# Hashed attention with a mixture of adapters: sign rows read over 16 partitions, loads behind them, and a new order for the first pair

## The chip, the cores and the metric

The kernel runs on one core of one Trainium2 chip. The metric is the device time of one execution in microseconds (us). A profile of one execution gives the span from its first to its last instruction, which is a little shorter: 193.1 us in an execution of 195.3 us.

## The reference, cut to what matters

Attention over 4 batches x 8 heads with 768 positions of 64 dimensions. Queries and keys are hashed to six bits each, and a query sees only keys with the same six bits. The output of all heads, 3072 rows of 512, then goes through a top-2 mixture of eight rank-16 adapters.

```python
q_bits = (np.einsum('bhsd,dk->bhsk', q, proj) > 0)        # proj: 64 x 6
k_bits = (np.einsum('bhsd,dk->bhsk', k, proj) > 0)
mask   = q_bucket[:, :, :, None] == k_bucket[:, :, None, :]
scores = np.where(mask, scale * q @ k.T, -1e9)
attn   = softmax(scores)                                  # sum + 1e-09
out    = attn @ v
# ... then, on x = out as 3072 x 512:
logits = x @ w_gate                                       # 8 experts, the best 2 are taken
delta  = sum over the 2 of  w * ((x @ A[e]) @ B[e])
return x + delta
```

## The kernel before: the parts that the change touches

The heads are taken in 16 pairs. For a pair, `aug` holds queries and keys, transposed, in rows 0 to 63, and six rows of signs (+ or - times a scale) and one constant row in rows 64 to 70. One matmul over 71 rows then gives the score plus a large negative number wherever a bit differs, so the mask costs nothing more, and the exponential turns those to zero. `aug[:, t, h, i, :]` is row block t (6 of them), head h, and i = 0 for queries, 1 for keys.

A pair is nine steps `s`. Each step makes 1024 columns of scores, an exponential on ScalarE, and carries other work along: that of the pair before (values, normalisation, adapters) and of the next two pairs (loads, casts, transposes, hashes, signs).

```python
def score(self, p, s, ...):
    ps = self.ps_s.tile([P, 1024], F32, tag="s", ...)
    # 2 or 3 matmuls of 256 or 512 columns:
    nc.tensor.matmul(out=ps[:, o:o + w], lhsT=aug[0:71, kt, h, 1, :], rhs=aug[0:71, ..., h, 0, :], ...)
    nc.scalar.activation(out=self.P_[p][:, s * 1024:end], in_=ps, func=ACT.Exp, ...)
```

The signs of a later pair take a way through memory. `turn32` transposes 32 x 32 blocks on VectorE, `hash` multiplies by the projection on TensorE, `sign` makes the signs on VectorE and writes them to a scratch tensor in device memory, and `signs` reads them back into rows 64 to 70 of `aug`:

```python
def sign(self, p, r0=0, r1=128):
    # ... signs into s2, [128, T, 32] bf16
    if p not in self.dr:
        self.dr[p] = self.scr.tile([T, P, 32], BF16, tag="dr", name=f"dr{p}")
    nc.sync.dma_start(out=self.dr[p].rearrange("t p c -> p t c")[r0:r1], in_=s2[r0:r1])

def signs(self, p, js=None):
    aug = self.aug[p % 3]
    if js is None:
        nc.sync.dma_start(out=aug[64:71].rearrange("b t h i c -> b (t h i) c"),
                          in_=self.dr[p].rearrange("t (j b i) c -> b (t j) (i c)", j=4, b=8)[0:7])
        return
    # ... else one of four quarters at a time
```

Queries and keys come by `loadqk` (384 KB each), are cast to bf16 by GpSimd (`natcast`), and transposed by a DMA (`xbar`) into all 128 rows of the head-0 half of `aug`, of which rows 64 to 127 are head 1. `shift`, on VectorE, moves these to rows 0 to 63 of the head-1 half, and only after it may the sign rows be written.

```python
def slot(self, p, s):
    n1, n2 = p + 1, p + 2
    self.score(p, s)
    if p == 0: self.first(s)
    self.pvs(p - 1, s + 9); self.pvs(p, s)
    if p > 0:
        if s in (0, 1): self.hash(n1, s)
        if s == 2: self.sign(n1)
        if s == 3:
            self.norm(p - 1, 1); self.to_bf(p - 1); self.shift(n1)
        if s == 4: self.signs(n1)
        if s == 6: self.turn(p - 1)
        if s == 2: self.loadv(n1)
    if s in (5, 6):
        self.natcast(n2, s - 5); self.xbar(n2, s - 5)
    if s == 7:
        self.loadqk(p + 3, 0); self.loadqk(p + 3, 1)
    # ... turn32 of n2 at 5 and 6, vcast of n1 at 7, norm(p, 0) at 8, the adapters
    if s == 3 and p >= 8 and p % 4 < 3:
        self.store(p // 4 - 2, p % 4)                     # 512 KB of output
```

All these DMAs are issued by SyncE, in the order in which they stand here, and SyncE waits in that order too.

Pair 0 has no pair before it, so `start` and `first` make its transposes and hashes on TensorE directly from the loads; `cast` fills rows 0 to 63 and `sign_here` the sign rows, on VectorE, one instruction for every half `e` of the row blocks. Here j = 0, 1 are queries and keys of head 0 and j = 2, 3 those of head 1.

```python
def first(self, s):
    v = self.hb if s else None
    if s == 0:
        v = self.hb = [self.ps_v.tile([self.P, 512], F32, tag="v", ...) for e in range(2)]
        self.cast(0, 2, "act"); self.hash_here(2, v)
        self.turn32(1, 0, 0); self.turn32(1, 1, 0)
    if s == 1:
        self.cast(1, 2, "act"); self.hash_here(3, v)
        self.sign_here(2, 0, v[0]); self.sign_here(2, 1, v[1])
    if s == 2:
        for f in range(2): self.hash(1, f, (0, 1))
        self.sign(1, 0, 64); self.loadv(1)
        self.sign_here(3, 0, v[0], 0, 1); self.sign_here(3, 1, v[1], 0, 1)
    if s == 3:
        self.turn32(1, 0, 1); self.turn32(1, 1, 1); self.shift(1)
        self.signs(1, (0, 1))
        self.sign_here(3, 0, v[0], 1, 3); self.sign_here(3, 1, v[1], 1, 3)
    if s == 4:
        for f in range(2): self.hash(1, f, (2, 3))
        self.sign(1, 64, 128)
    if s == 6: self.signs(1, (2, 3))
```

Of the kernel before, what the change touches and what calls it, by code (L numbers as in the profile page):

```python
# [12 lines left out]
F32 = mybir.dt.float32  # L13
# [6 lines left out]
class Emitter:  # L20


    def __init__(self, ctx, tc, q, k, v, proj, w_gate, A, Bm, out):
# [27 lines left out]
        self.sgp = pool("sgp", 2)  # L51
        self.scr = ctx.enter_context(tc.tile_pool(name="scr", bufs=2, space=bass.MemoryType.DRAM))
        self.pp = pool("pp", 2)
# [11 lines left out]
        self.nat, self.vn, self.P_, self.pv = {}, {}, {}, {}  # L65
        self.tr, self.hs, self.R, self.nb, self.dr = {}, {}, {}, {}, {}
        self.x, self.xb, self.xT, self.lz = {}, {}, {}, {}
# [3 lines left out]
    def consts(self):  # L71
        nc, P, T, D, S = self.nc, self.P, self.T, self.D, self.S
        sg = self.singles
        self.wz = sg.tile([P, 512], BF16, name="wz")
        nc.vector.memset(self.wz, 0.0)
        self.dume = sg.tile([P, 1], F32, name="dume")
        nc.scalar.activation(out=self.dume, in_=self.wz[:, 0:1], func=ACT.Exp)
        self.ident = sg.tile([P, P], F32, name="ident")
        make_identity(nc, self.ident)
        self.proj3 = sg.tile([P, 32], F32, name="proj3")  # L80
        nc.vector.memset(self.proj3, 0.0)
        self.aug = [sg.tile([P, T, 2, 2, P], BF16, name=f"aug{i}") for i in range(3)]
        self.vb = [sg.tile([P, 2, T + 1, D + 1], BF16, name=f"vb{i}") for i in range(3)]
        for j in range(4):
            nc.vector.memset(self.aug[0][64:96, :, j // 2, j % 2, :], 1.0 if j % 2 == 0 else -1.5)
        self.eps = sg.tile([P, P], BF16, name="eps")
        nc.gpsimd.memset(self.eps, 2.0 ** -56)
        self.ident_bf = sg.tile([P, P], BF16, name="ident_bf")
        nc.gpsimd.tensor_copy(out=self.ident_bf, in_=self.ident)
        self.wa = sg.tile([P, self.nD, self.LZ], BF16, name="wa")  # L90
        self.Bcat = sg.tile([self.ER, self.Dm], BF16, name="Bcat")

# [94 lines left out]
    def sign(self, p, r0=0, r1=128):  # L187
# [7 lines left out]
        nc.vector.tensor_scalar(out=s2[r0:r1], in0=sg, scalar1=self.ssc[r0:r1], scalar2=None, op0=ALU.mult)  # L195
        if p not in self.dr:
            self.dr[p] = self.scr.tile([T, P, 32], BF16, tag="dr", name=f"dr{p}")
        nc.sync.dma_start(out=self.dr[p].rearrange("t p c -> p t c")[r0:r1], in_=s2[r0:r1])

    def signs(self, p, js=None):  # L200
# [4 lines left out]
        if js is None:  # L205
            nc.sync.dma_start(out=aug[64:71].rearrange("b t h i c -> b (t h i) c"),
                              in_=self.dr[p].rearrange("t (j b i) c -> b (t j) (i c)", j=4, b=8)[0:7])
            return
        src = self.dr[p].rearrange("t (j b i) c -> b j t (i c)", j=4, b=8)[0:7]
        for j in js:  # L210
            nc.sync.dma_start(out=aug[64:71, :, j // 2, j % 2, :], in_=src[:, j])

# [57 lines left out]
    def sign_here(self, j, e, tile, u0=0, u1=3):  # L270
        r = 64 + 32 * (j % 2)
        self.nc.vector.tensor_scalar(out=self.augv(slice(64, 70), j, e)[:, u0:u1],
                                     in0=tile[r:r + 6, 0:384].rearrange("p (u c) -> p u c", u=3)[:, u0:u1],
                                     scalar1=0.0, scalar2=0.5, op0=ALU.is_gt, op1=ALU.subtract)

# [257 lines left out]
    def start(self):  # L533
# [7 lines left out]
        self.loadqk(0, 0, 1, nc_s)  # L541
        self.loadqk(0, 1, 1, nc_a)
        self.loadqk(1, 0)
        self.loadqk(1, 1)
# [8 lines left out]
        h = [self.ps_s.tile([self.P, 2, 512], F32, tag="s", name=f"h{j}") for j in range(2)]  # L553
        h = [(t[:, 0], t[:, 1]) for t in h]
        for j in (0, 1):
            for u in range(3):
                self.T1(j, u, j == 1)
        warm(1)
        self.tcopy(0)
        self.tcopy(1, "act")  # L560
        self.hash_here(0, h[0])
        self.hash_here(1, h[1])
        self.cast(0, 0)
        self.cast(1, 0, "act")
        self.cast(0, 1, "act")
        self.cast(1, 1, "act")
        self.sign_here(0, 0, h[0][0])
        self.sign_here(0, 1, h[0][1])
        self.sign_here(1, 0, h[1][0], 0, 1)
        self.sign_here(1, 1, h[1][1], 0, 1)  # L570
        for j in (2, 3):
# [12 lines left out]
        self.vcast(0)  # L584
        self.sign_here(1, 0, h[1][0], 1, 3)
        self.sign_here(1, 1, h[1][1], 1, 3)

    def first(self, s):
        v = self.hb if s else None
        if s == 0:  # L590
            v = self.hb = [self.ps_v.tile([self.P, 512], F32, tag="v", name=f"hb{e}") for e in range(2)]
            self.cast(0, 2, "act")
            self.hash_here(2, v)
            self.turn32(1, 0, 0)
            self.turn32(1, 1, 0)
        if s == 1:
            self.cast(1, 2, "act")
            self.hash_here(3, v)
            self.sign_here(2, 0, v[0])
            self.sign_here(2, 1, v[1])  # L600
        if s == 2:
            for f in range(2):
                self.hash(1, f, (0, 1))
            self.sign(1, 0, 64)
            self.loadv(1)
            self.sign_here(3, 0, v[0], 0, 1)
            self.sign_here(3, 1, v[1], 0, 1)
        if s == 3:
            self.turn32(1, 0, 1)
            self.turn32(1, 1, 1)  # L610
            self.shift(1)
            self.signs(1, (0, 1))
            self.sign_here(3, 0, v[0], 1, 3)
            self.sign_here(3, 1, v[1], 1, 3)
        if s == 4:
            for f in range(2):
                self.hash(1, f, (2, 3))
            self.sign(1, 64, 128)
        if s == 6:
            self.signs(1, (2, 3))  # L620

    def pvs(self, p, s):
# [5 lines left out]
        if p == 0:  # L628
            own = {6: [(A, -1), (A, 0), (A, 1)], 7: [(A, 2), (A, 3)], 8: [(A, 4), (A, 5)],
                   9: [(B, -1), (B, 0), (B, 1)], 10: [(B, 2), (B, 3)], 11: [(B, 4), (B, 5)]}  # L630
        for (d, h), k in own.get(s, ()):
# [5 lines left out]
    def slot(self, p, s):  # L637
# [6 lines left out]
        if p > 0:  # L644
            if s in (0, 1):
                self.hash(n1, s)
            if s == 2:
                self.sign(n1)
            if s == 3:
                self.norm(p - 1, 1)  # L650
                self.to_bf(p - 1)
                self.shift(n1)
            if s == 4:
                self.signs(n1)
            if s == 6:
                self.turn(p - 1)
            if s == 2:
                self.loadv(n1)
        if s in (5, 6):
            self.natcast(n2, s - 5)  # L660
            self.xbar(n2, s - 5)
        if s == 7:
            self.loadqk(p + 3, 0)
            self.loadqk(p + 3, 1)
        t = 4 if n2 == self.N - 1 else 5
# [4 lines left out]
        if n2 == self.N - 1:  # L670
# [4 lines left out]
            if s == 8:  # L675
                self.sign(n2)
                self.vcast(n2)
        if (p, s) == (1, 0):
            self.norm(0, 0)
        if s == 8 and p > 0:  # L680
            self.norm(p, 0)
        if p > 0:
            self.moe(p, s)
        if s == 3 and p >= 8 and p % 4 < 3:
            self.store(p // 4 - 2, p % 4)

# [26 lines left out]
    def late(self, g):  # L713
# [11 lines left out]
        if g == 2:  # L725
            self.shift(q)
            self.signs(q)
            self.store(b - 2, 2)
        if g == 3:
# [140 lines left out]
```

## Time and profile before

| | before |
|---|---|
| device time, median of three (lowest, highest) | 196.92 us (193.67, 197.64) |
| span of the profiled execution | 193.1 us |
| ScalarE busy | 149.2 us, 77% |
| TensorE busy (PE) | 169.9 us, 88% |
| VectorE busy | 119.3 us, 62% |
| GpSimd busy | 100.3 us, 52% |
| DMA queue of SyncE, share of 16 engines | 69.3% |
| mean granted TensorE clock | 0.885 |

PE is matmuls, PEld the weight loads that overlap them, DVE is VectorE, ACT ScalarE, POOL GpSimd, SP SyncE. A "q" after the name stands for the engine's sequencer, which waits and issues DMAs. In a group of instructions, "out<-in" names the tiles written and read; after the bar come busy time, mean nanoseconds of one, then the idle time of the engine just before these instructions and what ended most of it. A matmul at a lower granted clock counts as busy for longer, so a busy PE is not a PE at its peak. The span falls into a start up to the first exponential at 8.77 us, fourteen pairs of nine steps, 18 steps for the last two pairs together (from 160.7 us), and a tail after the last exponential of them (from 179.3 us).

### The profile page before, as it was taken

To read this page: it belongs to the slowest core of one execution; us is meant where nothing else is said; L and a number is where in the kernel's file an instruction comes from. 1 tells how busy PE (TensorE), PEld (TensorE's weight loads), DVE (VectorE), ACT (ScalarE), POOL (GpSimd) and SP (SyncE) were. 2 spreads that over 40 slices of the span, in tenths; PEclk is the share of its full clock that TensorE was granted. 3 is DMA by queue.
4 is the path that set the end of the run, shared out by engine and by line. 5 is a ranking of instruction groups with operands and counts; after the bars stand their busy time and mean duration, and the time that the engine had idled before them with its cause. 6 is when DMAs were issued, how large, how long until landed. Compare 5 with 4: busy or idle time off the path is not lost.

```text
span 193.1 us, 5252 instructions
## 1 busy us (share of the span) xinstructions
PE 169.9 (88%) x2116; PEld 110.9 (57%) x2116; DVE 119.3 (62%) x331; ACT 149.2 (77%) x170; POOL 100.3 (52%) x148
## 2 busy tenths in 40 slices
PE   7989989897999999899959999699978999989750
PEld 3425665665466758475735767367552677879410
DVE  7879564645144767687934487476880728586750
ACT  3797897989567999898955799658993489988540
POOL 3798276959374465556551906446171475111190
PEclk9999999999657999999995899958995589999955
DMA  5864588999979687876994998947597591415025
GB/s 156 289 208 99 128 248 222 154 210 142 198 153 119 208 124 240 102 243 107 283 219 132 240 194 202 253 102 100 164 225 218 111 250 26 160 70 219 2 109 221
DMA packets 58542, 33.06 MB, mean 171 GB/s; under 512 B 44310, under 2 KB 56726, under 8 KB 58518
## 3 DMA queue, kind: packets, MB, share of 16 engines
q1 hardware_dynamic: 53254, 31.80, 69.3%
q0 software_dynamic: 4832, 0.27, 4.6%
q10 hardware_dynamic: 432, 0.66, 0.9%
q8 instruction: 16, 0.26, 0.6%
q14 instruction: 8, 0.07, 0.1%
HBM read 20.06 MB, written 7.03 MB: 140 GB/s over the span
## 4 chain that ended last, share of the span: by engine, by line
PE 65%; DMA 17%; ACT 8%; DVE 4%; issue 2%; POOL 1%; POOLq 1%; SPq 0%; DVEq 0%; ACTq 0%
PE s L299 31%; DMA aug<-dr 14%; PE pv L330 13%; PE hs L183 8%; ACT P L306 6%; DMA dr<-s 3%; PE lz L433 3%; PE dl L502 3%; PE pv L318 2%; PE warm L551 2%; PE xtp L369 1%; PE pv_u L387 1%; ACT acc L512 1%; ACT aug L258 1%; PE hb L266 1%
## 5 line engine op out<-in xcount | busy, mean ns | idle before, releaser
L306 ACT ACTIVATE P<-s 128x1024 bf16<-128x1024 f32 x144 | 139.8, 1027 | 29.7 <-PE s L299 28.6
L299 PE MATMUL s<-aug 71*128 71x256 bf16 (+1 forms) x408 | 95.4, 342 | 12.2 <-DMA aug<-dr 10.0
L330 PEld LDWEIGHTS <-P 128*128 128x128 bf16 x1008 | 49.9, 103 | 16.7 <-issue 4.8
L299 PEld LDWEIGHTS <-aug 71*128 71x128 bf16 x408 | 34.8, 102 | 35.6 <-issue 14.3
L330 PE MATMUL pv<-vb,P 128*128 128x65 bf16 x1008 | 52.8, 201 | 0.0
L359 POOL CAST xb<-x 128x768 bf16<-128x768 f32 x14 | 16.5, 1177 | 56.6 <-DVE x L350 53.8
L173 DVE STREAM_TRANSPOSE R<-nat 128x768 f32<-128x768 f32 (+1 forms) x32 | 29.1, 918 | 1.3 <-DMA nat<-in_q_dram 0.9
L219 POOL CAST nb<-nat 128x768 bf16<-128x768 f32 x30 | 24.4, 836 | 1.5 <-DMA nat<-in_k_dram 0.9
L192 DVE TENSOR_SCALAR hs<-hs 128x192 f32<-128x192 f32 (+1 forms) x16 | 5.8, 362 | 24.6 <-PE hs L183 24.5
L183 PE MATMUL hs<-R,hst 128*32 128x192 f32 x240 | 18.6, 366 | 0.3 <-DVE R L173 0.3
L515 DVE SCALAR_TENSOR_TENSOR acc<-dl,rt,x 128x512 f32<-128x512 f32 x20 | 14.6, 739 | 5.0 <-PE dl L502 4.9
L159 POOL CAST vb<-vn 128x768 bf16<-128x768 f32 x16 | 13.3, 830 | 6.7 <-DMA vn<-in_v_dram 6.3
L350 DVE TENSOR_TENSOR x<-pv,ri 128x384 f32<-128x384 f32 x28 | 15.6, 558 | 1.0
L370 DVE COPY xT<-xtp 128x768 bf16<-128x768 bf16 x14 | 7.8, 556 | 13.3 <-PE xtp L369 13.0
L161 POOL TENSOR_TENSOR vs<-vn 128x384 f32<-128x384 f32 x16 | 15.9, 993 | 0.0
L502 PE MATMUL dl<-Bcat,zT 128*128 128x512 bf16 x24 | 10.1, 437 | 2.2 <-ACT zT L493 0.8
L433 PE MATMUL lz<-wa,xT 128*128 128x136 bf16 x96 | 10.7, 242 | 0.7 <-ACT xT L422 0.5
L183 PEld LDWEIGHTS hs<-R,hst 128*32 128x32 f32 x240 | 5.5, 112 | 8.7 <-issue 6.6
L318 PE MATMUL pv<-vb,eps 128*128 128x390 bf16 x28 | 10.1, 361 | 0.0
L233 DVE COPY aug<-aug 64x1536 bf16<-64x1536 bf16 x15 | 8.9, 595 | 0.5
L409 POOL CAST xb<-x 128x256 bf16<-128x256 f32 x5 | 2.0, 400 | 12.3 <-DVE x L406 12.3
L164 POOL TENSOR_TENSOR vb<-vs,vs 128x128 bf16<-128x128 f32 x16 | 7.3, 457 | 1.3
(70 smaller groups left out, 141.1 us busy)
## 6 DMA issues: line engine op xcount, KB each, us to landing
vn<-in_v_dram SPq DMA_DIRECT2D x16, 384.0 KB
nat<-in_q_dram SPq DMA_DIRECT2D x15, 384.0 KB
nat<-in_k_dram SPq DMA_DIRECT2D x15, 384.0 KB
out_dram<-acc SPq DMA_DIRECT2D x10, 512.0 KB
out_dram<-acc SPq DMA_DIRECT2D x3, 256.0 KB
dr<-s SPq DMA_DIRECT2D x14, 48.0 KB
aug<-dr SPq DMA_DIRECT2D x14, 42.0 KB
aug<-nb SPq DMA_TRANSPOSE x30
```

Of the source, the lines that this page charges most:

```text
L161: nc.gpsimd.tensor_add(out=s3, in0=vn[:, :, 0:3, :], in1=vn[:, :, 3:6, :])
L173: self.nc.vector.transpose(out=self.R[p][:, i, hs, :], in_=self.nat[p][:, i, hs, :])
L183: nc.tensor.matmul(out=self.hs[p][32 * j:32 * j + 32, 0:6], lhsT=self.hst[:, hf].rearrange("p b i -> p (b i)"), rhs=rhs, start=(hf == 0), ...
L219: self.nc.gpsimd.tensor_copy(out=self.nb[p][:, i].rearrange("p t h d -> p h t d"), in_=self.nat[p][:, i].rearrange("p h (t d) -> p h t d", ...
L299: nc.tensor.matmul(out=ps[:, o:o + w], lhsT=aug[0:71, kt, h, 1, :], rhs=rhs, start=True, stop=True)
L306: nc.scalar.activation(out=self.P_[p][:, s * 1024:end], in_=ps, func=ACT.Exp, scale=128.0 if p == 0 else 0.125)
L330: self.nc.tensor.matmul(out=pv[:, i, :], lhsT=self.P_[p][:, o:o + P], rhs=vb[:, h, kt, :], start=False, stop=(kt == T - 1), skip_group_che ...
L350: nc.vector.tensor_tensor(out=self.x[b][:, :, c:c + D], in0=pv[:, :, 0:D], in1=ri.unsqueeze(2).to_broadcast([P, T, D]), op=ALU.mult)
L359: self.nc.gpsimd.tensor_copy(out=xb, in_=self.x[b][:, :, hp * P:(hp + 1) * P])
L433: nc.tensor.matmul(out=self.lz[b, I][:, I.index(i), :], lhsT=self.xT[b][:, t, i, :], rhs=self.wa[:, t, :], start=(t == 0 and i == I[0]), s ...
L502: self.nc.tensor.matmul(out=ps, lhsT=self.zT[b, i][0], rhs=self.Bcat, start=True, stop=True)
L515: nc.vector.scalar_tensor_tensor(out=acc, in0=dl, scalar=rt, in1=x, op0=ALU.mult, op1=ALU.add)
```

## The change

It has two sides. For the pairs from 1 on, the read of the sign rows takes 16 partitions of `aug` (64 to 79) instead of 7, from a scratch tensor that has one more row so that the last partitions have something to read; rows 71 to 79 are not used by any matmul. The order on SyncE's queue changes with it: the loads of q and k for three pairs ahead come right behind the sign read and ahead of the two transposes, and the store of output moves from between sign write and sign read to the end of the pair before. The shift stands ahead of the normalisation. This is to keep other transfers out of the way of the sign read, which the next pair's first score needs.

For pair 0, the two hash products of head 1 are made one after the other, into different rows of the same two tiles, and all of head 1's signs are made ahead of pair 1's; the signs of head 0 become one instruction for both halves; a cast goes from ScalarE to VectorE. Pair 1's second head is hashed and read later, and the value matmuls of pairs 0 and 1 move by about a step. One warm-up matmul is left out.

```diff
-        self.scr = ctx.enter_context(tc.tile_pool(name="scr", bufs=2, space=bass.MemoryType.DRAM))
+        self.scr = ctx.enter_context(tc.tile_pool(name="scr", bufs=1, space=bass.MemoryType.DRAM))
+        self.drs = [self.scr.tile([T + 1, P, 32], BF16, name=f"dr{i}") for i in range(2)]
 ...
-        nc.sync.dma_start(out=self.dr[p].rearrange("t p c -> p t c")[r0:r1], in_=s2[r0:r1])
+        nc.sync.dma_start(out=self.drs[p % 2][0:T].rearrange("t p c -> p t c")[r0:r1], in_=s2[r0:r1])
+
+    def drsrc(self, p):
+        a = self.drs[p % 2][0:1].rearrange("o p c -> o (p c)")
+        return bass.AP(a.tensor, a.offset, [[128, 16], [1024, 4 * self.T], [1, 128]])
 ...
-            nc.sync.dma_start(out=aug[64:71].rearrange("b t h i c -> b (t h i) c"),
-                              in_=self.dr[p].rearrange("t (j b i) c -> b (t j) (i c)", j=4, b=8)[0:7])
+            nc.sync.dma_start(out=aug[64:80].rearrange("b t h i c -> b (t h i) c"), in_=self.drsrc(p))
 ...  (the quarters of pair 1: 16 partitions for queries, 7 for keys)
 ...  (start)
-        warm(1)
-        self.sign_here(0, 0, h[0][0])
-        self.sign_here(0, 1, h[0][1])
-        self.sign_here(1, 0, h[1][0], 0, 1)
-        self.sign_here(1, 1, h[1][1], 0, 1)
+        self.sign_here(0, None, h[0])
+        self.sign_here(1, None, h[1], 0, 1)
 ...  (first)
         if s == 0:
-            self.cast(0, 2, "act")
-            self.hash_here(2, v)
         if s == 1:
+            self.hash_here(2, v)
+            self.hash_here(3, v)
             self.cast(1, 2, "act")
-            self.hash_here(3, v)
+            self.cast(0, 2)
             self.sign_here(2, 0, v[0])
             self.sign_here(2, 1, v[1])
+            self.sign_here(3, 0, v[0], 0, 1)
+            self.sign_here(3, 1, v[1], 0, 1)
         if s == 2:
             for f in range(2):
                 self.hash(1, f, (0, 1))
+            self.sign_here(3, 0, v[0], 1, 3)
+            self.sign_here(3, 1, v[1], 1, 3)
             self.sign(1, 0, 64)
 ...
-            self.signs(1, (0, 1))
+            self.signs(1, (1, 0))
+            self.loadqk(3, 0)
-        if s == 4:
+        if s == 6:
             for f in range(2):
                 self.hash(1, f, (2, 3))
             self.sign(1, 64, 128)
-        if s == 6:
-            self.signs(1, (2, 3))
+            self.loadqk(3, 1)
+        if s == 8:
+            self.signs(1, (3, 2))
 ...  (pvs: the value matmuls of pair 0 start at step 7 instead of 6 and end at 12, those of pair 1 follow)
 ...  (slot)
             if s == 2:
                 self.sign(n1)
+                self.loadv(n1)
             if s == 3:
+                self.shift(n1)
+            if s == (3, 4)[p == 1]:
                 self.norm(p - 1, 1)
                 self.to_bf(p - 1)
-                self.shift(n1)
 ...
         if s in (5, 6):
+            if s == 5 and p > 0:
+                self.loadqk(p + 3, 0)
+                self.loadqk(p + 3, 1)
             self.natcast(n2, s - 5)
             self.xbar(n2, s - 5)
-        if s == 7:
-            self.loadqk(p + 3, 0)
-            self.loadqk(p + 3, 1)
 ...
-        if s == 3 and p >= 8 and p % 4 < 3:
-            self.store(p // 4 - 2, p % 4)
+        if s == 8 and n1 >= 8 and n1 % 4 < 3:
+            self.store(n1 // 4 - 2, n1 % 4)
 ...  (late: one store taken out, since slot does it)
```

## The prediction

> **What bounds the kernel now.** I read the page first: slices, then groups. In the slices the row PEclk shows the TensorE clock that was granted; in the groups two lines matter, the exponentials on ScalarE (L306) and the score matmuls (L299).
>
> ```profile
> PEclk9999999999657999999995899958995589999955
> L306 ACT ACTIVATE P<-s 128x1024 bf16<-128x1024 f32 x144 | 139.8, 1027 | 29.7 <-PE s L299 28.6
> L299 PE MATMUL s<-aug 71*128 71x256 bf16 (+1 forms) x408 | 95.4, 342 | 12.2 <-DMA aug<-dr 10.0
> ```
>
> The reader is to see three things. The 144 exponentials are 139.8 us of a 193.1 us span, so ScalarE is the engine that could fill the span. It stood idle 28.6 us because scores were late. The scores were late for 10.0 us because the sign rows of `aug` had not been read back (`aug<-dr`). And the clock falls to a half or so in four stretches in the middle.
>
> The third view is the timeline of ScalarE, which gives the start of each pair's first exponential, and from it the windows of one pair each (start:end, length, then busy time of PE, PEld, DVE, ACT and POOL, then granted clock, DMA share, GB/s). Pairs 5 to 9:
>
> ```profile
> 62.30:71.35 9.05, 9.02 (x140) 6.12 (x132) 5.82 (x21) 8.87 (x12) 5.46 (x7) 1.00 0.81 172
> 71.35:80.64 9.29, 8.55 (x131) 6.13 (x127) 7.33 (x29) 8.72 (x11) 5.44 (x7) 1.00 0.85 183
> 80.64:89.70 9.06, 8.88 (x129) 5.85 (x126) 7.59 (x15) 8.64 (x9) 4.74 (x6) 1.00 0.72 169
> 89.70:100.67 10.97, 8.82 (x128) 5.73 (x124) 7.36 (x14) 8.66 (x10) 6.14 (x9) 1.00 1.03 221
> 100.67:112.85 12.18, 12.15 (x141) 7.66 (x140) 5.83 (x20) 8.93 (x11) 5.45 (x7) 0.72 0.86 176
> ```
>
> A pair in which nothing goes wrong takes 9.05 to 9.29 us, with ScalarE busy 8.6 to 8.9 of it. Pair 8 has the same work on every engine and takes 10.97. Pair 9 takes 12.18 with PE busy all through at clock 0.72: there TensorE is the bound, because it is slow. So the end is set by ScalarE where all goes well, by a sign read at the head of a pair, or by a slow TensorE after it. The fourth view, the chain of waits around the end of pair 8, and the fifth, SyncE's queue in it, show which:
>
> ```profile
> 94.23 0.45 PE s L299 x3
> 94.93 4.99 DMA aug<-dr
> 99.97 0.61 PE s L299 x3
> ```
>
> ```profile
> 92.44 0.37 SPq L198 DMA_DIRECT2D dr<-s  x1
> 92.84 0.55 SPq L151 DMA_DIRECT2D vn<-in_v_dram  x1
> 93.44 0.47 SPq L531 DMA_DIRECT2D out_dram<-acc  x1
> 94.93 0.29 SPq L206 DMA_DIRECT2D aug<-dr  x1
> 95.32 2.79 SPq L225 DMA_TRANSPOSE aug<-nb  x2
> 98.17 1.13 SPq L143 DMA_DIRECT2D nat<-in_q_dram  x1
> 99.34 0.46 SPq L143 DMA_DIRECT2D nat<-in_k_dram  x1
> ```
>
> The sign read is issued at 94.93, behind a 384 KB load of V and a 512 KB store, with two DMA transposes 0.4 us behind it, and the next pair's scores start at 99.97. In pair 1 (26.91) and pair 2 (36.13) the same read, without a store, took 2.41 and 2.39 us in the chain; in pair 7 3.31; in the three pairs with a store ahead and the wait visible 4.99, 5.09 and 5.46.
>
> **What the Trainium skill says.** "TensorE: Matmul & The Clock Gate", section "HAM oscillation — how this bites in real kernels": a TensorE gap longer than about 3.4 us brings the clock back to half. The trace fits: the chain's waits of 4.99 us (94.93), 5.09 us (117.68), 5.46 us (140.20) and the 3.16 + 3.57 us of write and read at 41.74 to 48.54 are each followed by a window of clock 0.61 to 0.72, and those of 2.4 and 3.3 us are not. (TensorE still has some work in these gaps, so the fit is in which gaps, not in a bare length.) "DMA: Bandwidth & Descriptors", section "Why a DMA increments its semaphore by 16 and not by 1": a queue spreads a transfer over the largest number of engines up to 16 that divides the slowest dimension, so 7 partitions use 7 engines and 16 use 16. The trace does not name engines, so no view here shows it. Same page, section "Queues, rings and completion order": an engine takes descriptors in order, and the completion mark lands only after that engine's earlier writes. So what stands ahead of the sign read in the queue, and on the same engines, delays it; 2.4 us against 5 us with a store ahead agrees.
>
> **The change, part by part.** (a) *Order on SyncE.* Per pair the queue was sign write, V load, (store), sign read, transpose, transpose, q load, k load. It becomes sign write, V load, sign read, q load, k load, transpose, transpose, (store). No work is added but bytes: the read grows from 42.0 KB to 16 x 24 x 256 B = 98 KB, the same 24 pieces per partition. I work out a pair from its first score at 0. The sign write is issued at about +3.3 (32.53 - 29.36 = 3.2 in pair 2, 92.44 - 89.05 = 3.4 in pair 8) and its read follows 1.5 to 3.6 us later, when the write has landed (66.67 - 64.56 = 2.1; 36.13 - 32.53 = 3.6). So the read is issued at +5.4 to +6.9 and, at 2.4 us, ready at +7.8 to +9.3. A pair is 9.15 us long. So with nothing heavy ahead and no transposes close behind, the read is just in time nearly always. (b) *Stores* go out at the end of the pair before, some 2 us ahead of the next sign write; 512 KB at the 400 GB/s that the DMA view shows around 96 us is 1.3 us of transfer, mostly over by then.
>
> The gain: pairs 2 to 13 take, from the ScalarE timeline, 160.7 - 30.07 = 130.6 us. At (9.21 + 9.05 + 9.29 + 9.06) / 4 = 9.15 us they would take 109.8. So 20.8 us at most: the waits at the heads of pairs, and the slow clock that follows four of them (49.30 to 62.30 took 13.00 us, 100.67 to 112.85 took 12.18, 123.52 to 135.75 took 12.23, 146.84 to 160.70 took 13.86).
>
> (c) *Pair 0.* Its nine exponentials take 8.77 to 19.85 = 11.08 us. Two lines, of ScalarE and of VectorE:
>
> ```profile
> 16.10 4.71 ACT L306 ACTIVATE P<-s 128x1024 bf16<-128x1024 f32 x5 [1.15 <-PE s L299]
> 15.83 0.77 DVE L272 TENSOR_SCALAR aug<-hb 6x256 bf16<-6x256 f32 x2
> ```
>
> ScalarE waited 1.15 us for scores that waited for the last signs of head 1, queued on VectorE behind pair 1's signs, transposes and shift. These signs now come first, both hash products one after the other, and one of two casts (0.52 us each on ScalarE) goes to VectorE. That is 1.15 + 0.52 = 1.7 us less on ScalarE; the two merged sign instructions for head 0 save VectorE perhaps 0.3 us more. In return pair 1's second-half signs are hashed at step 6 instead of 4 and read at step 8 instead of 6; they are used in the middle of pair 1. I count 1.2 us gained. (d) *Pair 1* took 10.22 us, of which 0.98 was the wait in front of pair 2: 0.8 us gained.
>
> The most that can be had is thus 20.8 + 1.2 + 0.8 = 22.8 us. I take off 0.3 us in each of the twelve pairs (3.6 us) for reads that come at +9.3 rather than +7.8, and 3 us for one slow-clock stretch that stays (a stretch like pair 9 costs 12.18 - 9.15 = 3.0). That leaves 16.2 us. The last two pairs (18.6 us for 18 exponentials) and the tail (13.80 us after 179.3) are as before. 196.92 - 16.2 = 180.7; I say 180.
>
> **The rivals.** *A late transpose takes the place of the late sign read.* The transposes now stand behind 768 KB of loads. If the loads are issued at +6 and take 3.7 us, the transposes land at about +12, that is +3 in the next pair, and the shift that needs them stood at +4 (33.38 - 29.36). VectorE's order has the shift ahead of the normalisation now, so a late shift also delays the bf16 copy, the next cast on GpSimd and so the next transpose: a loop from pair to pair. For it: the DMA view shows about 1.4 us near 99 in which next to nothing is moved, with transposes in flight. Against it: VectorE has 1.5 to 4 us idle in each pair and no idle time before the shift is listed now. It would make some 0.5 to 1 us a pair, time 186 to 190. *The read is no faster, only wider.* More than twice the bytes, on all engines instead of few, waits for the slowest of them. Then the non-store pairs stay as they are and only the three stores gain, with the clock stretches behind them: about (10.97 - 9.15) + (10.67 - 9.15) + (11.09 - 9.15) = 5.3 us plus 3 x 3 us, time 183. *The clock falls anyway.* If TensorE's slow stretches come from something else than these waits, 20.8 shrinks by the excess of pairs 4, 9, 11 and 13, 3.9 + 3.0 + 3.1 + 4.7 = 14.7, and only some 6 us are won, time 191.
>
> **Range and chances.** All clean gives 196.92 - 22.8 = 174; the worst rival that I believe 191. I put the 80% range at 172 to 190. The executions before lie between 193.67 and 197.64, so even the third rival would be near 3% faster. Faster by over 2%: 0.88; within 2%: 0.08; slower: 0.04, for a loop of late transposes worse than I see.
>
> **What would show it right or wrong.** Right: PE's wait for `aug<-dr` falls from 10.0 to under 3 us; the windows of pairs 2 to 13 come near 9.15 us each; the granted clock stays at 1.00 between 20 us and the last pairs; ScalarE's wait on scores falls from 28.6 to about 12 us; the 1.15 us in pair 0 is gone. Wrong: new idle time on VectorE ahead of the shift ended by `aug<-nb`, a read that still takes 4 to 5 us in the chain, or half-clock stretches that no wait precedes.

## The result and the profile after

| | before | after |
|---|---|---|
| device time, median (lowest to highest), runs | 195.69 us (193.67 to 197.64), 4 | 188.40 us (186.73 to 191.94), 4 |
| span of the profiled execution | 193.1 us | 185.2 us |
| pairs 0 and 1, pairs 2 to 13 | 21.3 us, 130.6 us | 21.7 us, 121.9 us |
| half-clock time between 8 and 165 us | 34.1 us | 13.7 us |

The ratio is 0.964, with a 95% interval of 0.957 to 0.971: about 7 us are won, where 16 were predicted. Ratios with an interval compare only executions within 1.5% of the fastest of their kernel; every other time is a median of all executions. The pairs are read from the starts of the exponentials as in the prediction. The half-clock time is summed from the clock records of the trace; tail and last pairs are left out of it, since their clock falls in every kernel here.

The page after, in the three lines that answer to those of before (clock in 40 slices; exponentials; scores):

```profile
PEclk9996999999998589999999999999699999999955
L314 ACT ACTIVATE P<-s 128x1024 bf16<-128x1024 f32 x144 | 139.6, 1028 | 23.0 <-PE s L307 21.2
L307 PE MATMUL s<-aug 71*128 71x256 bf16 (+1 forms) x408 | 89.1, 324 | 12.7 <-ACT P L314 5.2
```

ScalarE's wait for scores fell from 28.6 to 21.2 us, not to 12. Three slow stretches are left, at 14.7, 59.1 and 130.8 us. The list of waits (us in total, times, longest):

```profile
ACT P L314 <- PE s L307: 21.2, 30, 2.0
...
DVE aug L237 <- DMA aug<-nb: 9.8, 10, 2.2
...
PE s L307 <- DMA aug<-dr: 3.6, 4, 1.5
```

TensorE's own wait for signs is down to 3.6 us (the weight loads of the same matmuls, counted apart, stand in the same four waits, for 4.0 us), and VectorE has a new wait of 9.8 us for the transposes, which the prediction named as a sign of its first rival. Neither is 21.2 us. Windows of pairs 4 to 6, columns as in the prediction:

```profile
49.36:59.36 10.00, 8.46 (x124) 5.64 (x120) 4.97 (x10) 8.55 (x10) 6.95 (x11) 0.99 1.03 182
59.36:71.56 12.20, 12.17 (x145) 7.65 (x142) 5.70 (x20) 9.01 (x10) 5.08 (x7) 0.73 0.83 158
71.56:80.43 8.87, 8.66 (x135) 6.13 (x127) 6.84 (x26) 8.74 (x12) 4.10 (x5) 1.00 0.67 175
```

The middle pair is the old picture: PE busy all through at clock 0.73. What came ahead of it, in SyncE's queue, in the chain, and on PE (start, us, and in brackets the idle time before):

```profile
51.83 0.37 SPq L197 DMA_DIRECT2D dr<-s  x1
52.24 0.55 SPq L152 DMA_DIRECT2D vn<-in_v_dram  x1
53.86 0.33 SPq L209 DMA_DIRECT2D aug<-dr  x1
54.24 0.46 SPq L144 DMA_DIRECT2D nat<-in_q_dram  x1
```

```profile
53.86 4.74 DMA aug<-dr
58.65 0.62 PE s L307 x3
```

```profile
56.75 0.35 PE L338 MATMUL pv<-vb,P 128*128 128x65 bf16 x6
58.65 0.62 PE L307 MATMUL s<-aug 71*128 71x512 bf16 x3 [1.54 <-DMA aug<-dr]
```

No store stands ahead of this read, and yet it took 4.74 us; TensorE stood still for 1.54 us, and the clock fell 0.5 us later, for 6.8 us. The DMA part of the page says that this read was no exception (last number: median us from the issue to the landing, which is the last update of the transfer's semaphore); the sign write ahead of it stands below:

```profile
aug<-dr SPq DMA_DIRECT2D x14, 96.0 KB, 3.8
dr<-s SPq DMA_DIRECT2D x14, 48.0 KB, 2.1
```

The prediction had put 2.4 us there for the read.

### The profile page after: what moved, and what is told of

Read it like the earlier page. It is cut to its first block, busy times and chain, and to the rows that moved or that the text cites. A ratio compares the mean times of both kernels' runs of the same rounds, so it can differ in the third digit from the quotient of the medians.

```text
span 185.2 us, 5244 instructions
## 1 busy us (share of the span) xinstructions
PE 158.9 (86%) x2115; PEld 105.0 (57%) x2115; DVE 116.8 (63%) x329; ACT 148.4 (80%) x169; POOL 95.1 (51%) x148
## 4 chain that ended last, share of the span: by engine, by line
PE 47%; ACT 20%; DMA 16%; DVE 5%; POOL 3%; issue 3%; POOLq 1%; SPq 0%; ACTq 0%; DVEq 0%
PE s L307 22%; ACT P L314 18%; DMA aug<-dr 7%; PE pv L338 7%; PE hs L184 6%; DMA aug<-nb 6%; PE lz L441 3%; DMA vn<-in_v_dram 2%; PE dl L510 2%; PE warm L561 2%; PE pv_u L395 1%; PE pv L326 1%; DVE aug L282 1%; DMA dr<-s 1%; ACT aug L262 1%
## 5 line engine op out<-in xcount | busy, mean ns | idle before, releaser
L314 ACT ACTIVATE P<-s 128x1024 bf16<-128x1024 f32 x144 | 139.6, 1028 | 23.0 <-PE s L307 21.2
L307 PE MATMUL s<-aug 71*128 71x256 bf16 (+1 forms) x408 | 89.1, 324 | 12.7 <-ACT P L314 5.2
L338 PEld LDWEIGHTS <-P 128*128 128x128 bf16 x1008 | 46.6, 99 | 13.7 <-issue 1.2
L307 PEld LDWEIGHTS <-aug 71*128 71x128 bf16 x408 | 33.4, 98 | 37.1 <-issue 23.1
L338 PE MATMUL pv<-vb,P 128*128 128x65 bf16 x1008 | 49.8, 196 | 0.0
L367 POOL CAST xb<-x 128x768 bf16<-128x768 f32 x14 | 11.5, 822 | 57.1 <-DVE x L358 44.4
L184 PE MATMUL hs<-R,hst 128*32 128x192 f32 x240 | 18.2, 365 | 0.0
L441 PE MATMUL lz<-wa,xT 128*128 128x136 bf16 x96 | 9.9, 229 | 0.7 <-ACT xT L430 0.5
L164 POOL TENSOR_TENSOR vs<-vs 128x128 f32<-128x128 f32 x16 | 7.5, 467 | 1.3
```

The costliest lines, as they stand in the source:

```text
L184: nc.tensor.matmul(out=self.hs[p][32 * j:32 * j + 32, 0:6], lhsT=self.hst[:, hf].rearrange("p b i -> p (b i)"), rhs=rhs, start=(hf == 0), ...
L338: self.nc.tensor.matmul(out=pv[:, i, :], lhsT=self.P_[p][:, o:o + P], rhs=vb[:, h, kt, :], start=False, stop=(kt == T - 1), skip_group_che ...
L441: nc.tensor.matmul(out=self.lz[b, I][:, I.index(i), :], lhsT=self.xT[b][:, t, i, :], rhs=self.wa[:, t, :], start=(t == 0 and i == I[0]), s ...
```

## The experiments

The theory: the read of 16 partitions is the slower one, it lands late, TensorE stands still, and the clock falls for it. Rivals: the loads of q and k right behind the read; V's load ahead of it; the late transposes; the new start; a clock that falls by itself. All times are medians in us with lowest and highest. The kernel before ran beside every set of kernels, and its time drifts between the sets, so each row has its own. "Gaps" counts TensorE's idle gaps over 1 us between 9 and 165 us of the profiled execution.

| kernel | time | before, beside it | profiled span | half clock | gaps |
|---|---|---|---|---|---|
| a_seven | 182.27 (178.34 to 185.28) | 191.41 | 183.5 | 17.1 | 5 |
| a_loads_late | 197.31 (195.59 to 373.63) | 191.41 | 193.8 | 34.1 | 8 |
| b_stores | 187.94 (180.63 to 193.40) | 191.41 | 178.8 | 0 | 6 |
| a_old_start | 190.54 (187.00 to 195.85) | 191.41 | 188.3 | 10.2 | 7 |
| after_again | 189.19 (180.95 to 198.39) | 194.13 | 196.6 | 34.1 | 7 |
| a_vearly | 192.39 (189.69 to 199.26) | 194.13 | 190.5 | 23.9 | 7 |
| a_seven_oldstart | 180.98 (179.16 to 189.38) | 194.13 | 177.4 | 0 | 1 |
| a_best1 | 192.35 (189.69 to 195.50) | 194.13 | 191.7 | 27.3 | 6 |
| a_start7 | 182.77 (179.91 to 187.85) | 190.75 | 181.4 | 10.2 | 4 |
| old_start_again | 181.37 (178.28 to 190.29) | 190.75 | 179.6 | 6.8 | 5 |
| b_wide | 198.47 (195.73 to 202.72) | 190.75 | 200.5 | 44.4 | 7 |
| b_fill | 186.12 (183.76 to 187.02) | 190.75 | 182.9 | 0 | 1 |
| a_fill | 190.00 (186.37 to 192.39) | 189.92 | 187.6 | 3.4 | 2 |
| o7_fill | 185.72 (183.37 to 191.08) | 189.92 | 182.9 | 0 | 1 |
| s7_fill | 185.68 (184.67 to 187.34) | 189.92 | 183.3 | 0 | 2 |

**The width alone.** a_seven is the changed kernel with one line undone (pair 1's quarters stay wide):

```diff
-  nc.sync.dma_start(out=aug[64:80].rearrange(...), in_=self.drsrc(p))
+  nc.sync.dma_start(out=aug[64:71].rearrange(...),
+      in_=self.drs[p % 2][0:T].rearrange("t (j b i) c -> b (t j) (i c)", j=4, b=8)[0:7])
```

> The changed kernel with the sign read of pairs 2 to 15 back to 7 partitions (168 pieces of 256 bytes instead of 384), order and all else as changed. Theory crowding (the wide read has more pieces, which are dealt out together with the pieces of the loads right behind it, so that the read takes 4 to 5 us instead of 2.4): the waits for the sign read in the chain fall from 4.2 to 4.7 us to 2.5 to 3, TensorE's wait for it from 3.6 us to under 1.5, time 184 to 186 us. Rival late transposes (the read is innocent, what costs is that the transposes now stand behind the loads, 9.8 us of VectorE's waiting ahead of the shift): nothing changes, 187 to 189. Rival spread (16 engines are what makes the read quick; on 7 it would queue behind the loads): 190 or more.

It took 182.27 us, against 188.40 and 189.19 of the changed kernel; counted from the kernel before beside it, it is 9.1 us down, the changed kernel 7.3 and 4.9. So the one line is worth some 2 to 7 us, which the drift between the sets doesn't let one say more closely from this run alone. TensorE's wait for signs did not fall under 1.5 us as expected: it is 3.7 us in two waits, 2.5 of them for pair 1's first quarter, which stays wide, and 1.2 for a read of 7 partitions that took 4.40 us (issued at 57.48); a third gap, of 2.15 us, ends as the read issued at 114.55 lands after 5.08 us. A cleaner pair, with the start of before in both, comes below: a_old_start at 190.54 us and a_seven_oldstart at 180.98 and 181.37 differ in this one line, and are 0.9, 13.2 and 9.4 us under the kernel before beside them.

b_wide is the other way round, the kernel before with nothing but that read widened:

```diff
-  nc.sync.dma_start(out=aug[64:71].rearrange(...), in_=self.dr[p].rearrange(...)[0:7])
+  nc.sync.dma_start(out=aug[64:80].rearrange(...), in_=self.drsrc(p))     # and the longer scratch tensor
```

> The kernel before with only the read of the signs widened to 16 partitions (384 pieces for 168), loads and stores where they were. If the wide read is itself the faster one, as the prediction took it to be no slower, its median from issue to landing stays at or under that of before and the time is 0.97 to 1.00. If it is slower whenever V's load is still under way, the landing rises to 3.0 us or more where no store is ahead, and the ratio is 1.00 to 1.03.

198.47 us, 7.7 over the kernel before beside it (184.68 to 195.96); its lowest execution, 195.73, is just under the highest of that. Here nothing is moved behind the read, so the width does harm by itself. Its chain and its clock:

```profile
27.23 3.31 DMA aug<-dr
...
50.04 4.31 DMA aug<-dr
...
61.28 3.52 DMA aug<-dr
```

```profile
PEclk9999995559999559999998559999998569999997
```

These are the reads for pairs 2, 4 and 5, with no store about. The read for pair 2 took 2.41 us in the kernel before. Within that read, counting the trace's records of 256-byte pieces in order from the issue, the 168th ended 1.37 us after it in the kernel before and the 384th 1.70 us after it here; the rest of the difference is between the last piece and the landing, 1.0 us against 1.6. The Trainium skill, "DMA: Bandwidth & Descriptors", section "Why a DMA increments its semaphore by 16 and not by 1", says that a transfer over k engines has its other 16 - k increments written at once. The semaphore records fit: with 7 partitions a read has eight updates, the first 0.46 us after the issue, and with 16 partitions sixteen, here the first 3.2 us after it. So the wide read does wait for all sixteen engines.

The same records give the landing of every read of 7 partitions, which the page leaves out. Medians of the 14 reads, wide against narrow in kernels that are otherwise close: 3.8 and 4.1 us in the two profiles of the changed kernel against 3.0 in a_seven; 3.9 in a_old_start against 3.0 and 2.8 in a_seven_oldstart and old_start_again. So a narrow read is quicker by about 1 us, but in this order it doesn't land in 2.4 us either, and single ones took up to 5.1.

**The loads behind the read.** a_loads_late puts q and k back behind the transposes and keeps the wide read:

```diff
-            if s == 5 and p > 0:
-                self.loadqk(p + 3, 0); self.loadqk(p + 3, 1)
             self.natcast(n2, s - 5); self.xbar(n2, s - 5)
+        if s == 7 and p > 0:
+            self.loadqk(p + 3, 0); self.loadqk(p + 3, 1)
```

> The changed kernel with the q and k loads back behind the two transposes; the wide read, the moved stores and the start stay. Theory crowding: the read is followed by two transposes only, which start slowly, so it takes 2.4 to 3 us and the chain's waits for it fall; the transposes land about 2.5 us after issue, so VectorE's wait for them before the shift falls from 9.8 to under 2 us; time 183 to 186. Rival transposes behind the read are what made it slow before (4 to 5 us in the pairs with a store): the waits for the sign read come back, 191 to 194.

197.31 us, slower than the changed kernel, although VectorE's wait for the transposes fell from 9.8 to 0.9 us and the reads' landing from 3.8 to 3.3. So neither the loads behind the read nor the late transposes are what was missing, and the order of the loads is a gain of the change. (One of its four executions took 373.63 us at full clock; it was not profiled, and its cause is unknown.)

**V's load ahead of the read.** In a_vearly, V is loaded a pair earlier, behind the transposes; a_best1 does the same with 7-partition reads and the old start:

```diff
-                self.loadv(n1)          # behind the sign write, at step 2
+            if s == 6 and n2 < self.N - 1:
+                self.loadv(n2)          # behind the transposes, one pair earlier
```

> The changed kernel with the 384 KB load of V moved from between sign write and sign read to behind the transposes, one pair earlier; the read stays 16 partitions wide. In the changed kernel the reads that were issued 2.3 us or more after the V load landed in 2.5 to 3.0 us and those issued 2.1 us or less after it in 3.2 to 5.1 us. If the pieces of V that are still in the queues are what slows the wide read, the median from issue to landing falls from 3.8 to 2.5 to 2.8 us and the time by 3 to 6 us. If only the q and k loads behind it do, it stays at 3.5 or more.

> All three: 7 partitions, V a pair earlier, old start; loads behind the read and stores moved as in the changed kernel. If crowding of the sign read is the main cost, the sign reads land in about 2.4 us with nothing but loads behind, no TensorE gap over 1.4 us is left in pairs 2 to 13, the clock stays up: 174 to 180 us, 0.90 to 0.92 of the time before. If late transposes bind, VectorE's wait for them stays at 10 us or grows and the time is not under 182.

192.39 and 192.35 us: no gain. a_best1 is clearly worse than the same without the moved load (180.98, highest 189.38, against a lowest of 189.69); a_vearly overlaps with the changed kernel beside it (189.19). The page of a_vearly:

```profile
aug<-dr SPq DMA_DIRECT2D x14, 96.0 KB, 2.8
dr<-s SPq DMA_DIRECT2D x14, 48.0 KB, 3.1
```

The read did fall to the 2.8 us that I expected, but the load now stands directly ahead of the sign write, whose landing rose from 2.1 us by the same amount. In a_best1 the reads landed in 2.5 us in the median and the writes in 3.1, five of the 16 in 4.0 to 4.7. The queueing was moved from the read to the write, and the signs need both.

**The stores alone.** The kernel before with only the stores moved:

```diff
-        if s == 3 and p >= 8 and p % 4 < 3:
-            self.store(p // 4 - 2, p % 4)
+        if s == 8 and p + 1 >= 8 and (p + 1) % 4 < 3:
+            self.store((p + 1) // 4 - 2, (p + 1) % 4)
```

> The kernel before with one thing changed: the five stores that stood between sign write and sign read go out at the end of the pair before. If the stores are the main cause of the waits of 5 us and of the slow clock after them, about 5.3 us of waits and up to 9 us of slow clock go: 182 to 186 us. If the transposes behind the read are, only the queueing of 1.3 us behind each store goes, and the waits of 3.3 us and more stay: 191 to 195.

Three of the five reads that had a store ahead (in pairs 8, 9 and 10), in its chain:

```profile
93.43 2.38 DMA aug<-dr
...
103.49 2.39 DMA aug<-dr
...
113.62 2.39 DMA aug<-dr
```

The other two landed in 2.39 and 2.55 us; in the kernel before, the five took 4.61 to 5.46. That part of the prediction holds. The gain in time is less sure: the median of 187.94 us missed the expected 182 to 186, and its range overlaps with that of the kernel before beside it (186.30 to 197.65). The profiled execution, with a span of 178.8 us, had no slow stretch before the last pairs; others of the same kernel went up to 193.40.

**The start.** a_old_start is the changed kernel with the start of before (wide reads, pair 3's loads at step 7); a_seven_oldstart has the 7-partition read as well:

```diff
-  # start, first, sign_here and pvs of the changed kernel
+  # ... of the kernel before; q and k of pair 3 at step 7 of pair 0
```

> The changed kernel with pair 0 and pair 1 as before (hashes, signs, casts, value matmuls, the warm-up matmul). The prediction counted 1.2 us of gain in pair 0. If the new start is worth that, this is 1 to 2 us slower than the changed kernel, 189 to 190. If the half clock at 14.7 to 18.2 us in the changed kernel comes from the new start and eats its gain (pair 0 took 11.47 us against 11.08), this is as fast or up to 1 us faster, 187 to 188.5, with the clock at 1.00 through pairs 0 and 1.

> The changed kernel with the read of 7 partitions and with pairs 0 and 1 as before. In the changed kernel with 7 partitions TensorE waited 2.5 us for pair 1's first sign read (17.9 to 20.4 us) and then had a half clock; pairs 0 and 1 took 23.9 us against 21.3 before. If the new start only moves the wait to pair 1's read, the old start gives 1 to 2.5 us: 0.93 to 0.945 of the time before, pairs 0 and 1 about 21.3 us. If the old start costs what the prediction said, it is 1.2 us slower than the kernel with 7 partitions and the new start.

The first took 190.54 us, so the start was not the missing gain. The second took 180.98 us, the lowest median of all. It ran again as old_start_again, beside a_start7, the new start with narrow quarters and nothing pushed in between them:

```diff
-            self.signs(1, (1, 0)); self.loadqk(3, 0)
+            self.signs(1, (1, 0)); self.loadv(1)             # V from ahead of the quarters
 ...
-            self.loadqk(3, 1)
-            self.signs(1, (3, 2))
+            self.signs(1, (3, 2)); self.loadqk(3, 0); self.loadqk(3, 1)
```

> The changed kernel with 7-partition sign reads everywhere, and in the new start the V load of pair 1 and the q and k loads of pair 3 put behind the quarter reads of pair 1 instead of between them. If the new start itself is sound and only its late first quarter cost it time, pairs 0 and 1 together take 20.0 to 20.8 us (21.4 with the old start, 21.7 in the changed kernel) and the ratio to the kernel before is 0.92 to 0.93. If the new start is the worse order anyway (exponentials of pair 0 that wait for corners of the hash, first value products a step later), the two pairs stay at 21.4 us or more and the ratio is no better than the 0.932 of the 7-partition reads with the old start.

> The 7-partition reads with the old start, q and k loads behind the sign read and moved stores, once more, beside the new start in the same call. 0.925 to 0.94 of the kernel before if the 0.932 was no chance of that call.

Pairs 0 and 1 took 20.8 us in a_start7, 9.46 and 11.34; the changed kernel has 21.7 and 23.6 in its two profiles, the old start with narrow reads 21.4 and 23.2. So pair 0 does gain, 1.6 us against the 11.08 of before, and pair 1 gives 1 us of it back: TensorE waits 1.5 us at 27.3 us, in front of pair 2. That wait is not the new start's alone: in old_start_again it is 3.0 us, and pair 1 takes 12.1. The ranges of the times, 182.77 and 181.37 in the median, overlap. In the changed kernel's own order, pair 1's first quarter comes late as well: five of the six profiles with the new start and wide quarters (a_seven, a_loads_late, after_again, a_vearly, a_fill) have a TensorE gap of 2.2 to 2.6 us at 17.6 to 18.0 us; a_start7 and s7_fill, with narrow quarters first, have none there. Waits and clock of the version at 180.98 us:

```profile
ACT P L310 <- PE s L303: 13.1, 25, 1.5
...
DVE aug L237 <- DMA aug<-nb: 11.6, 10, 2.4
```

```profile
PEclk9999999999999999999999999999999999999955
```

VectorE waits for late transposes even longer than in the changed kernel, in the fastest version of all, so that wait is not what held the changed kernel back. It isn't off the path everywhere, though. This version's chain passes through it once:

```profile
48.54 3.92 DMA aug<-nb
53.17 4.45 DMA aug<-dr
```

The late transposes delayed the shift and with it the sign read, which landed at 57.62, just ahead of the next scores at 57.67.

**The clock.** First the changed kernel once more, to see its spread:

> The changed kernel as it is, beside the kernel before and the other kernels of this set on one chip, to compare them. 0.95 to 0.98 of the time before.

180.95 to 198.39 us: one program, six executions, 17 us. Then idle matmuls, whose result nobody uses, at the end of each pair; in the kernel before (b_fill), in the changed one (a_fill), in a_seven_oldstart (o7_fill) and in a_start7 (s7_fill):

```diff
+        if s == 8 and p > 0:
+            w = self.ps_n.tile([self.P, 512], F32, tag="n", name=f"fill{p}")
+            for i in range(5):
+                self.nc.tensor.matmul(out=w, lhsT=self.wz[:, 0:128], rhs=self.wz, start=True, stop=True)
```

> The kernel before with five idle matmuls of 512 columns behind the last score of every pair from 1 on (their result is not used), which fill about 1.1 us of TensorE's wait for the signs; the wait itself stays. If the slow-clock stretches come from TensorE standing idle in that wait, they go (none between 20 and 160 us, at least two in the kernel before) and the time is 0.95 to 0.98. If they have another cause, they stay and the five matmuls cost up to 0.3 us a pair: 1.00 to 1.02.

> The changed kernel with five idle matmuls of 512 columns behind the last score of every pair from 1 on. If most of the missing gain is slow clock that follows TensorE's waits for the wide sign reads, the time falls to 180 to 184 us (0.94 to 0.96 of the kernel before) and no half-clock stretch is left between 20 us and the tail. If the waits themselves cost it, the clock stays full and the time stays at 186 us or more (0.965 or above).

> The version with 7-partition reads, the old start, loads behind the sign read and moved stores, with the same five idle matmuls a pair. Its waits for signs are mostly gone, so if its 179 to 190 us were spread by the clock alone, the highest run falls under 184 and the median to 178 to 181 (0.92 to 0.94); if the five matmuls stand in the way of real ones, which no longer wait, it goes up by 0.2 to 0.5 us a pair, to 183 to 187 us.

> The same with the new start (its quarter reads 7-partition, V and the q and k loads of pair 3 behind them). With the clock held, the difference of the two starts shows by itself: if the new start is worth what its profile shows (pairs 0 and 1 in 20.8 us for 21.4), this one is 0.5 to 1 us under o7_fill; if it is worth nothing, they are within 0.5 us.

In b_fill no transfer is moved, and yet the slow stretches before the last pairs are gone, four in the profile of before and none here. In all six executions the mean granted clock is 0.974 to 0.982, against 0.886 to 0.960 in the eleven of before beside it. Two of its windows:

```profile
68.49:78.38 9.89, 9.89 (x143) 6.71 (x140) 7.06 (x26) 8.95 (x11) 4.78 (x6) 1.00 0.69 175
78.38:88.22 9.84, 9.84 (x134) 6.30 (x131) 7.58 (x15) 8.69 (x10) 4.93 (x7) 1.00 0.68 166
```

Its median is 4.6 us under that of before, because the long executions are gone; the shortest ones, from 183.76 us, are no better than those of before, from 184.68. The windows show the price: PE is busy 9.84 of 9.84 us at full clock. A good pair has PE busy 8.5 to 9.1 of some 9.2 us, so there is little room, and the idle matmuls make TensorE the bound, some 0.65 us a pair. The other three show no gain: a_fill stayed at 190.00 with the clock full from 24 us on, so filling doesn't repair the changed kernel. o7_fill and s7_fill came to 185.72 and 185.68 (0.980 of before, 0.972 to 0.988, and 0.984, 0.978 to 0.990), worse than without. a_fill thus can't be used to split the shortfall into wait and clock. With the clock held, no difference between the two starts is to be seen.

## Why the prediction was wrong

*What sets the time.* Taken together, the 13 profiles without idle matmuls (before, after and eleven experiments) lie on one line: span = 178.0 + 0.49 x half-clock time, with a correlation of 0.96. A microsecond at half clock costs half a microsecond, and the profiles differ chiefly in how much of it they have. And the half-clock time goes with gaps. In all 17 profiles, TensorE gaps between 9 and 160 us (those that fall in a slow stretch not counted) had a slow stretch begin within 4.7 us of their start in 0 of 38 cases if they were 0.85 to 1.3 us long, in 10 of 26 from 1.3 to 1.7 us, in 4 of 6 from 1.7 to 2.0 us, and in 20 of 22 above. Of 35 slow stretches 34 had such a gap ahead. This is found in the records after the fact; b_fill, which filled the gaps and nothing else, is the test that it is a cause.

*(a), the sign read.* This is the step that failed: "the read is issued at +5.4 to +6.9 and, at 2.4 us, ready at +7.8 to +9.3". The issue was as predicted (53.86 is +5.2 in the pair whose first score starts at 48.66), the 2.4 us was not: the page has 3.8, the chain up to 4.74. I had measured the 2.4 us on a 7-partition read and carried it over to one of 16 partitions, as if more than twice the bytes in more than twice the pieces cost nothing. And I had taken the quickest: in the kernel before, the nine reads without a store landed in 2.4 to 3.8 us, 2.7 in the median. Of the 1.4 us between 2.4 and 3.8 the width makes 0.8; the other 0.6 stands in a_seven's narrow reads too, at 3.0. By the sum, pairs 2 to 13 should have taken 109.8 + 3.6 + 3 = 116.4 us. They took 121.9 and 131.4 in the two profiles of the changed kernel, and 114.9 to 119.3 in the four with narrow reads, of which a_seven_oldstart, at 180.98 and 181.37 us, comes near the 180 that I gave to the wide one. That it comes so near is partly luck, since its reads land in 3.0 us, its start is the old one, and the profile at 114.9 has no slow stretch in these pairs, where the sum had one. My second rival, "the read is no faster, only wider", was the nearest, and too mild: b_wide shows the width to cost 7.7 us where nothing else is changed.

*The slow-clock term.* "3 us for one slow-clock stretch that stays" was the other size that was off, and it hangs on the first. The changed kernel's two profiles have 13.7 and 34.1 us at half clock, 7 and 17 us by the line above. What part of the width's cost is slow clock can be estimated from the span and the mean granted clock of every execution: span x (1 - clock) is at most what the slow clock cost. In the means, it is 13.0 us of a span of 187.5 in the changed kernel (ten executions) and 10.7 of 180.3 in a_seven (four): 2.2 of 7.2 us. a_old_start against a_seven_oldstart gives 4.2 of 8.5, and b_wide against the kernel before 5.4 of 8.7. So by this estimate up to a third to three fifths of what the width costs is slow clock, and the rest the waits themselves.

I had taken the gap of 3.4 us that the Trainium skill names ("TensorE: Matmul & The Clock Gate", section "HAM oscillation — how this bites in real kernels") as agreeing with the trace, because I held it against the length of the read in the chain (4.99 us at 94.93). TensorE's own idle gap there is 2.15 us, since it has other work during the read. No gap of these 17 profiles reaches 3.4 us, the longest is 3.1, and of those above 2.0 us 20 of 22 were followed by a slow stretch; the measurement decides. A gap that was taken to be harmless below 3.4 us made one remaining stretch look like a cautious deduction.

*(b), the stores,* was right: 5 us to 2.4. *(c), pair 0,* was right in size where pair 1's quarters are narrow and no load stands between them (1.6 us in a_start7 against 1.2), but in the changed kernel's profile it was lost again. Its first seven exponentials run through to 15.64 us, and then (ScalarE, in brackets the idle time before):

```profile
16.58 1.02 ACT L314 ACTIVATE P<-s 128x1024 bf16<-128x1024 f32 x1 [0.94 <-PE s L307]
18.37 1.02 ACT L314 ACTIVATE P<-s 128x1024 bf16<-128x1024 f32 x1 [0.77 <-PE s L307]
```

The scores came slowly, in the stretch at half clock from 14.7 to 18.2 us; it is the one of the 35 with no gap over 0.85 us ahead, and its cause stays open. *(d), pair 1,* was wrong: "0.8 us gained" was nothing in the changed kernel (10.27 and 11.75 us, before 10.22) and a loss of 1 us in a_start7, since a wait in front of pair 2 stands there still.

*The rivals.* The late transposes came as foreseen, 9.8 us on VectorE, but did not decide the time: without them a_loads_late is slower, and with more of them a_seven_oldstart is the fastest. "The clock falls anyway" is wrong as it was put, for 34 of 35 falls have gaps ahead of them, but right in that it leaves one and the same kernel with a spread of up to 17 us.

*Still open:* whether the wide read lands late because of the number of its pieces or because it needs all sixteen engines, on each of which V's load may be waiting. With V out of the way the wide read (a_vearly, 2.8 us) is close to the narrow one (a_best1, 2.5), so V's load has most of the part; but that fits both. A narrow read in more pieces, which would tell the two apart, wasn't run.

## What to carry to other kernels

A small transfer on the critical path should be kept small: widening it for the sake of more engines gave it more pieces and more engines to wait for, and cost 7.7 us of 191 by itself. A duration taken from the old form of a transfer doesn't hold for the new form; where a change alters a term of the sum, that term is the one to doubt. In a kernel with TensorE nearly full, look for its idle gaps one by one, here those of 1.3 us and more, for besides the wait they can bring a slow clock that costs about as much again; and idle matmuls in the gaps help only where TensorE has room for them.

The lowest median here has the change without its widened read and without its new start (a_seven_oldstart; a_start7, with the new start, can't be told from it): stores out of the way, q and k loads ahead of the transposes, shift first.

## What the runs showed of the hardware that was not expected

Slow stretches come in steps of 3.4 us: 3.4, 6.8, 10.2 and 13.7 us long between 9 and 165 us. A gap between 1.3 and 2.0 us sometimes brings one and sometimes not (14 of 32). One program on one chip ran in 180.95 and in 198.39 us, with a mean granted clock of 0.951 and 0.889.
